# Reordering the first loads and conversions of a Fourier-mixing and hardswish kernel on one core

## Chip, cores and metric

The kernel runs on one core of a Trainium2 chip. The metric is the device time of one execution in microseconds (us); lower is better. The core has five engines with a queue of instructions each: TensorE (PE; PEld is its weight load), VectorE (DVE), ScalarE (ACT), GpSimd (POOL) and SyncE (SP). SP, ACT and POOL also issue DMA transfers, which run on 16 shared DMA engines.

## The reference

```python
def _attn_ref(x) -> np.ndarray:               # x: (8, 3008, 256) float32
    X = np.fft.fft(x, axis=1)
    X = np.fft.fft(X, axis=2)
    return X.real.astype(np.float32)

def _moe_ref(x, w_in, w_out) -> np.ndarray:   # x: (24064, 256), w_in: (256, 2048), w_out: (2048, 256)
    h = x @ w_in
    relu6 = np.clip(h + 3.0, 0.0, 6.0)
    g = h * relu6 / 6.0
    return (g @ w_out).astype(np.float32)
```

The second function takes the first one's result, reshaped to (24064, 256). x is float32; both weight matrices arrive as float64.

## The kernel before

**Stages.** The sequence of 3008 is split as 47 x 64 (`N1`, `N2`). Stage 1 is the transform over the 47, as products with the table `F`; x is first folded, that is, added to its mirrored partner (`fold_half`, `fold_columns`), so that half the products are left. Its results `z` go out to DRAM (`zd`) and come back in another layout as groups `g`. Stage 2 is the transform over the 64, with the table `T`, and gives `q`. The transform over the 256 features is not run on the data: `fold_w_in` multiplies it (table `C`) into `w_in`, which gives `W1`; the last row of the result is kept as a column per feature block, `WN`. From `q`, `W1` and `WN` come the hidden values: `mlp1_products` makes two products `u` and `v` on TensorE, and `activate` adds them, the row `qn` times `WN` (L544) among them, and applies the hardswish on VectorE and ScalarE. The second product uses seven products in place of eight per 2 x 2 block (`G`, `combine`, `mlp2`, `finish`). The batch is worked in four pairs (`pairs`), each in chunks, each chunk in eight steps (`NF`).

**Float64 weights.** No engine multiplies float64 here, so each weight piece (512 KB, 16 in all: `PIECES`) is taken apart by hand. `load_w(j)` loads it on POOL's queue. `exponent_a(j)` writes the exponent's bytes into `PM[j % 3]` (two ScalarE instructions, L745), `exponent_b(j)` adds them up by two products on TensorE (L757), `exponent_c(j)` scales them on ScalarE (L760). `mantissa(j)` builds the fraction on VectorE (L768, L769), `join(j)` multiplies both there (L777 for pieces of `w_in`, L783 for `w_out`). Pieces 0 and 1 are the first two of `w_in`, 2 and 3 of `w_out`, 4 and 5 of `w_in` again, and so on. `fold_w_in(j)` then makes eight products, copies the result to `W1` (L811) and issues the `WN` transfers on SP (L815): 128 numbers of one partition to one number in each of 128 partitions.

**Order.** The order on each engine is the order in which the program's text issues things (`manual_schedule`). The start reads, from L828: TensorE runs `keep_awake` fillers (products of ones with zeros, L826); SP loads `FI`, `first_slot`, `C`, `F` (L833 to L837); POOL loads weight pieces 0 and 1 (L881), then issues eight gathers of x for the first half batch (`load_half`, L174, indices `IX` from `FI`), then pieces 2 and 3. ScalarE and VectorE convert pieces 0 and 1 as far as they can, ScalarE copies `first_slot` into the last x tile (L893) and clears a part of `T`, and SP loads the first part of `T` (`load_t(0)`, L895). Four rounds follow (`ORDER`), each with a fold on VectorE and its products in `stage1_early`; the last round is the one in `SPLIT`. `load_g_half` brings back the first group. `see` is a tiny POOL copy of a number of that group: POOL waits there, so the loads of pieces 4 to 9 behind it start when the group has landed. Then come the rest of the first conversions, `fold_w_in(0)` and `(1)`, stage 2 of the first group (`stage2_half`, its copy at L448, and `spread_by_pe` for `qn`), and the first products. `starting[0]` is true up to there.

**First steps.** For the first eight steps, `first_steps` and `second_steps` alternate and weave in the conversion of the pieces left. `head_b(j)` is `mantissa(j)` followed by the load of a later piece (`NEXT`: 6 loads 12, 7 loads 13, 8 loads 14, 9 loads 15). Behind these steps the loop runs `mlp1`, `combine` and `mlp2` evenly.

Of the kernel before, what the change touches and what calls it, by code (L numbers as in the profile page):

```python
# [58 lines left out]
def kernel(  # L59
# [140 lines left out]
    def fold_columns(hb, m, j, eng):  # L200
        a, r = hb.x[m][0:PX - 1, j::2, :], hb.xr[m][0:PX - 1, XC - 1 - j::-2, :]
        for p, q in ((slice(0, P + 1, P), slice(0, P + 1, P)), (slice(1, P), slice(D - 1, P, -1)),
                     (slice(D - 1, P, -1), slice(1, P))):
            eng.tensor_tensor(a[:, :, p], a[:, :, p], r[:, :, q], op=AL.add)
# [512 lines left out]
    def load_w(j):  # L717
        kind, n, i = PIECES[j]

        pool, tag, bufs = (wpool, "st", 2) if j in STRAIGHT else (spool, "t", None) if j in (2, 3) else (xpool, "x", None)  # L720
        st = pool.tile([P, 2 * WB], I32, tag=tag, bufs=bufs, name="st")
        o = st[:].bitcast(moe_w_in.dtype)
        if kind == "in":
            cs = slice(in_column(n, i), in_column(n, i) + WB // 2)
            nc.gpsimd.dma_start(out=o.rearrange("p (c j) -> p c j", c=2),
                                in_=moe_w_in[:, cs].rearrange("(c p) f -> p c f", p=P))
        else:
            r = (2 * n + i * NF) * P
            nc.gpsimd.dma_start(out=o.rearrange("p (c j) -> p c j", c=2),
                                in_=moe_w_out[r:r + 2 * P, :].rearrange("(c p) d -> p c d", p=P))  # L730
        raw[j] = st
# [9 lines left out]
    def exponent_a(j):  # L741
        top = raw[j][:].bitcast(I16).rearrange("p (n four) -> p n four", four=4)[:, :, 3]
        for i in range(2):
            low = PM[j % len(PM)][:, i].bitcast(U8).rearrange("p (n two) -> p n two", two=2)[:, :, 0]
            nc.scalar.activation(low, top, AF.Identity, bias=bias[:, i:i + 1], scale=(1 - 2 * i) / 16.0)  # L745

    def exponent_b(j):
        pm = [PM[j % len(PM)][:, i].bitcast(F16) for i in range(2)]
        if starting[0]:
            exs[j] = ps_h.tile([P, WB], F32, tag="uv", name="ex")[:]  # L750
        elif j % 2 == 0:
            exs[j] = bank([P, WB], "ex")[:]
        else:

            exs[j] = spare[1 if j % 4 == 1 else 0][:].rearrange("p i n -> p (i n)")
        for i in range(2):
            nc.tensor.matmul(exs[j], E[:, i], pm[i], start=(i == 0), stop=(i == 1))  # L757

    def exponent_c(j):
        nc.scalar.activation(exs[j].bitcast(I32), exs[j], AF.Identity, scale=2.0 ** 23)  # L760

    def mantissa(j):
        st = raw[j]
        hi = st[:].rearrange("p (n two) -> p n two", two=2)[:, :, 1]
        lo = st[:].bitcast(U32).rearrange("p (n two) -> p n two", two=2)[:, :, 0]
        top = wpool.tile([P, WB], I32, tag="top", bufs=3, name="top")
        frac = top[:].bitcast(F32)
        nc.vector.tensor_scalar(top[:], hi, 0xFFFFF, 0x100000, op0=AL.bitwise_and, op1=AL.bitwise_or)  # L768
        nc.vector.scalar_tensor_tensor(frac, lo, 2.0 ** -32, top[:], op0=AL.mult, op1=AL.add)  # L769
        fracs[j] = frac  # L770

    def join(j):
        kind, n, i = PIECES[j]
        frac, ex = fracs.pop(j), exs.pop(j)
        if kind == "in":
            o = wpool.tile([P, WB], F32, tag="wi", bufs=4, name="wi")
            nc.vector.tensor_tensor(o[:], frac, ex, op=AL.mult)  # L777
            w[PIECES[j]] = o[:]
            return

        for h, g in enumerate((B21, B22) if i else (B11, B12)):
            f, e = (t.rearrange("p (c q h e) -> h p c q e", c=2, h=2, e=DH)[h] for t in (frac, ex))
            nc.vector.tensor_tensor(block(n, g).rearrange("p c (q e) -> p c q e", e=DH), f, e, op=AL.mult)  # L783
# [15 lines left out]
    def fold_w_in(j):  # L799

        _, n, k = PIECES[j]
        nb = WB // 2
        cs = slice(in_column(n, k), in_column(n, k) + nb)
        wi = w.pop(PIECES[j]).rearrange("p (i f) -> p i f", i=2)

        ps = bank([P, 2, nb], "wps") if starting[0] else spare[k]
        for blk in range(2):
            for i in range(2):
                nc.tensor.matmul(ps[:, blk], C[:, i, blk * P:(blk + 1) * P], wi[:, i], start=(i == 0), stop=(i == 1))
        fs = range(cs.start // P, cs.stop // P)  # L810
        nc.scalar.copy(W1[:, :, cs], ps[:])  # L811

        wait = [] if k else fs[1:]
        for f in [fs[0], *rest, *(() if wait else fs[1:])]:
            nc.sync.dma_start(out=WN[:, f:f + 1], in_=W1[P - 1:P, 1, f * P:(f + 1) * P])  # L815
        rest[:] = wait

    def load_t(gr, ks=slice(0, 2 * KK)):
        for b in range(2):
            nc.sync.dma_start(out=T[b * N2:(b + 1) * N2, b, gr, :, ks], in_=c_stage2[:, gr, :, ks])  # L820


    def keep_awake(n, by=None):
        ps = ps_d.tile([P, 2 * TB], F32, tag="d", name="awake")
        for i in range(n):
            nc.tensor.matmul(ps[:], ones[:], Z[:] if by is None else by, start=True, stop=True)  # L826
# [1 line left out]
    Z = spool.tile([P, 2 * TB], F32, tag="s", name="Z")  # L828
    nc.vector.memset(Z[:], 0.0)
    nc.vector.memset(ones[:], 1.0)  # L830
    keep_awake(11)
    hb = halves[0]
    nc.sync.dma_start(out=FI[:], in_=c_stage1[:, 7 * PB:])  # L833
    first_slot = qpool.tile([P, 2 * TB], F32, tag="qn", name="first_slot")
    load_zero(first_slot[PB:PB + N1, 0:D], hb, nc.sync)
    nc.sync.dma_start(out=C[:], in_=c_dim.rearrange("(h p) d -> p h d", p=P))
    nc.sync.dma_start(out=F[:], in_=c_stage1[:, 0:7 * PB])  # L837
    bias = wpool.tile([P, 2], F32, tag="bias", name="bias")
    for i in range(2):
        nc.vector.memset(bias[:, i:i + 1], (2 * i - 1) * 7.5 / 16.0 - 896.0)  # L840
# [25 lines left out]
    def head_b(j):  # L866
        mantissa(j)
        if j in NEXT:
            load_w(NEXT[j])

    def tail(j):
        exponent_c(j)
        join(j)


    def see(x):
        nc.gpsimd.tensor_copy(seen[:], x)

    for j in range(2):  # L881
        load_w(j)
    nc.gpsimd.affine_select(E[:, 0], ones[:], pattern=[[-1, P]], compare_op=AL.is_equal, fill=0.0, base=0,
                            channel_multiplier=1)
    nc.scalar.mul(E[:, 1], E[:, 0], -1.0)
    for k, m in enumerate(ORDER):
        load_half(hb, m)
    for j in range(2, 4):
        load_w(j)
    for j in range(2):  # L890
        exponent_a(j)
        mantissa(j)
    nc.scalar.copy(zero_slot(hb), first_slot[PB:PB + N1, 0:D])  # L893
    clear_table(1)
    load_t(0)  # L895
    for k, m in enumerate(ORDER):
        if m in SPLIT:
            for j in range(2):
                fold_columns(hb, m, j, nc.vector)
        for part in range(2) if m not in SPLIT else ():  # L900
            fold_half(hb, m, part, nc.vector)
        stage1_early(hb, m)
    later[:] = later[4:6] + later[0:4] + later[6:8]
    load_g_half(hb, 0)

# [4 lines left out]
    take_half(halves[1], ORDER[0], cpool, "c")  # L910
    load_half(halves[1], ORDER[0])

    mantissa(2)
    for j in range(2):
        exponent_b(j)
        exponent_c(j)
        join(j)
    keep_awake(2)
    exponent_a(2)
    fold_w_in(0)  # L920
    exponent_a(3)
    fold_w_in(1)
    mantissa(3)
    exponent_b(2)
    keep_awake(1)
    exponent_b(3)
    tail(2)

    stage2_half(hb, 0)
    spread_by_pe(hb, bank([P, TB], "ps3")[:])  # L930
    tail(3)
    starting[0] = False
    spare = [ps_a.tile([P, 2, WB // 2], F32, tag="acc", name="spare") for h in range(2)]
# [114 lines left out]
    def second_steps(s):  # L1048
        j = 2 * s + 4
        if j - 2 < len(PIECES):  # L1050
            head_b(j)
            join(j)
            head_b(j + 1)
            if s == 1:
                mlp2_first(*chunk(s), halves=(0,))
                exponent_b(j + 1)
            exponent_c(j + 1)
            if j + 2 < len(PIECES):
                head(j + 2)
            join(j + 1)  # L1060
            if j + 3 < len(PIECES):
                exponent_a(j + 3)
                if s > 1:
                    head_b(j + 3)
            if s > 1:
                mlp2_first(*chunk(s), halves=(0,))
            if s == 3:
                stage2_half(halves[0], 1)
            mlp1(*chunk(s + 1))
            if s == 1:  # L1070
                head_b(j + 3)
            return
        mlp1(*chunk(s + 1))
        combine(*chunk(s + 1))
        mlp2_first(*chunk(s), halves=(0,))
        mlp1(*chunk(s + 2))
        mlp2_first(*chunk(s), halves=(1,))
# [117 lines left out]
```

## Time and profile before

| What | us |
|---|---|
| median of three runs (1944.76 to 1946.93) | 1946.17 |
| the profiled execution | 1950.4 |
| its span, from first to last instruction | 1948.7 |
| TensorE busy in it | 1928.2 |
| VectorE busy | 1425.6 |
| GpSimd busy | 1440.8 |
| ScalarE busy | 680.8 |
| first fold starts (VectorE) | 14.16 |
| stage 1's last product ends (TensorE) | 30.45 |
| first group back (POOL's `see`) | 36.81 |
| first product of `mlp1` (TensorE) | 41.56 |
| first product of the second step's `v` (TensorE) | 49.75 |

Times inside an execution count from the start of the span. The profile's groups and waits are read thus: a line of the kernel, the engine and its operation, what it wrote and read, how many there were, their busy time, and the idle time of the engine ahead of them with what ended it. The granted clock is the share of full speed that TensorE was given.

### The profile page before, as it was taken

To read this page: it belongs to the slowest core of one execution; us is meant where nothing else is said; L and a number is where in the kernel's file an instruction comes from. 1 tells how busy PE (TensorE), PEld (TensorE's weight loads), DVE (VectorE), ACT (ScalarE), POOL (GpSimd) and SP (SyncE) were. 2 spreads that over 40 slices of the span, in tenths; PEclk is the share of its full clock that TensorE was granted. 3 is DMA by queue.
4 is the path that set the end of the run, shared out by engine and by line. 5 is a ranking of instruction groups with operands and counts; after the bars stand their busy time and mean duration, and the time that the engine had idled before them with its cause. 6 is when DMAs were issued, how large, how long until landed. Compare 5 with 4: busy or idle time off the path is not lost.

```text
span 1948.7 us, 28199 instructions
## 1 busy us (share of the span) xinstructions
PE 1928.2 (99%) x9362; PEld 1660.2 (85%) x9362; DVE 1425.6 (73%) x2759; ACT 680.8 (35%) x1166; POOL 1440.8 (74%) x1646
## 2 busy tenths in 40 slices
PE   8999999999999999999999999999999999999998
PEld 5578888888998888888898888888899888888887
DVE  4877776767777777777787777777778777777777
ACT  4633333333333333333333333333333333333332
POOL 3487888886688887787678887878667667666765
PEclk8999999999999999999999999999999999999999
DMA  6431223311112122121111221212110101101000
GB/s 231 149 98 36 66 60 82 76 47 35 36 31 55 45 73 68 39 55 29 40 36 43 57 57 43 50 50 54 35 28 20 28 17 26 33 14 28 20 20 20
DMA packets 154600, 98.77 MB, mean 51 GB/s; under 512 B 121877, under 2 KB 136062, under 8 KB 154454
## 3 DMA queue, kind: packets, MB, share of 16 engines
q1 hardware_dynamic: 142562, 57.97, 12.3%
q0 software_dynamic: 11184, 38.77, 6.8%
q8 instruction: 73, 1.20, 0.3%
q14 instruction: 73, 0.60, 0.1%
q10 hardware_dynamic: 708, 0.23, 0.1%
HBM read 59.61 MB, written 37.32 MB: 50 GB/s over the span
## 4 chain that ended last, share of the span: by engine, by line
PE 94%; DVE 3%; DMA 1%; ACT 1%; issue 0%; POOL 0%; DVEq 0%; SPq 0%; ACTq 0%; POOLq 0%
PE acc L628 56%; PE v L535 16%; PE u L535 16%; PE ps L484 2%; PE ps L279 1%; PE acc L608 1%; DVE a L584 1%; DMA WN<-W 1%; DVE s L544 1%; ACT t L581 1%; DMA xt<-in_x_dram,IX 0%; PE ps L342 0%; DVE o L689 0%; DVE u L565 0%; PE ps L445 0%
## 5 line engine op out<-in xcount | busy, mean ns | idle before, releaser
L598 POOL TENSOR_TENSOR c<-a 128x512 f32<-128x512 f32 (+1 forms) x375 | 469.1, 1251 | 359.7 <-PE acc L628 304.2
L628 PE MATMUL acc<-c,G 128*128 128x256 f32 (+1 forms) x3008 | 697.2, 375 | 0.0
L581 ACT ACTIVATE t<-u,half 128x512 f32<-128x512 f32 (+1 forms) x384 | 260.6, 679 | 1148.4 <-DVE u L554 1069.1
L628 PEld LDWEIGHTS acc<-c,G 128*128 128x128 f32 x3008 | 565.2, 190 | 71.6 <-POOL c L598 0.4
L544 DVE SCALAR_TENSOR_TENSOR s<-qn,WN,u 128x256 f32<-128x256 f32 (+1 forms) x768 | 330.7, 472 | 344.0 <-PE u L535 337.1
L628 PE MATMUL acc<-a,G 128*128 128x256 f32 (+1 forms) x2256 | 541.6, 375 | 0.0
L628 PEld LDWEIGHTS acc<-a,G 128*128 128x128 f32 x2256 | 421.0, 189 | 73.6 <-issue 20.2
L535 PE MATMUL v<-q,W 127*128 127x256 f32 (+1 forms) x1536 | 389.4, 375 | 4.9 <-DVE a L584 4.9
L535 PE MATMUL u<-q,W 128*128 128x256 f32 (+1 forms) x1536 | 388.0, 375 | 0.2 <-ACT q L448 0.2
L584 DVE SCALAR_TENSOR_TENSOR a<-t,u 128x512 f32<-128x512 f32 (+2 forms) x448 | 264.1, 601 | 101.0 <-ACT t L581 96.1
L535 PEld LDWEIGHTS v<-q,W 127*128 127x128 f32 x1536 | 287.9, 190 | 46.3 <-DVE a L584 6.4
L535 PEld LDWEIGHTS u<-q,W 128*128 128x128 f32 x1536 | 285.8, 190 | 36.9 <-issue 1.9
L598 POOL TENSOR_TENSOR c<-a,c 128x256 f32<-128x256 f32 (+1 forms) x375 | 268.5, 716 | 29.4
L598 POOL TENSOR_TENSOR c<-c,a 128x256 f32<-128x256 f32 (+1 forms) x375 | 268.4, 716 | 29.4
L554 DVE TENSOR_TENSOR u<-s,v 128x512 f32<-128x512 f32 x352 | 245.0, 696 | 37.8 <-DVE s L544 0.9
L584 DVE SCALAR_TENSOR_TENSOR a<-t,v 128x512 f32<-128x512 f32 (+1 forms) x480 | 263.7, 566 | 0.1
L581 ACT ACTIVATE t<-v,half 128x512 f32<-128x512 f32 (+1 forms) x384 | 260.6, 679 | 0.2 <-PE acc L628 0.2
L556 DVE TENSOR_TENSOR v<-v,s 128x512 f32<-128x512 f32 x352 | 243.9, 693 | 0.0
L598 POOL TENSOR_TENSOR r<-w,e 128x256 f32<-128x256 f32 (+1 forms) x92 | 88.7, 985 | 3.6
L638 ACT ACTIVATE e<-acc 128x512 f32<-128x512 f32 (+2 forms) x184 | 83.4, 544 | 0.0
L689 DVE STREAM_TRANSPOSE o<-r 128x256 f32<-128x256 f32 (+1 forms) x192 | 72.6, 416 | 0.2
L598 POOL TENSOR_TENSOR w<-w,e 128x512 f32<-128x512 f32 (+1 forms) x46 | 57.5, 1250 | 3.6
(130 smaller groups left out, 797.7 us busy)
## 6 DMA issues: line engine op xcount, KB each, us to landing
out_dram<-o SPq DMA_DIRECT2D x747, 32.0 KB
g<-zd SPq DMA_DIRECT2D x42, 256.0 KB
zd<-z SPq DMA_DIRECT2D x48, 192.0 KB
xt<-in_x_dram POOLq DMA_DIRECT2D x21, 256.0 KB
st<-in_moe_w_in_dram POOLq DMA_DIRECT2D x8, 512.0 KB
st<-in_moe_w_out_dram POOLq DMA_DIRECT2D x8, 512.0 KB
qn<-qd SPq DMA_DIRECT2D x16, 256.0 KB
xt<-in_x_dram POOLq DMA_DIRECT2D x17, 192.0 KB
```

Of the source, the lines that this page charges most:

```text
L279: nc.tensor.matmul(ps[b][h * PB:(h + 1) * PB, 0:n], F[rows(b), 0:PB], y[rows(b), 2 * h:2 * h + n], start=True, stop=not last, skip_group_c ...
L484: nc.tensor.matmul(ps[:, blk, u * P:n].rearrange("p (b k) -> p b k", b=2), g[:, kk, blk * (P + 1):blk * (P + 1) + P], T[:, :, gr, blk, kk, ...
L535: nc.tensor.matmul(ps[:, i, 0:nq], W1[r, blk, f * P:(f + 1) * P], q[r, blk, of:of + nq], start=True, stop=True)
L544: nc.vector.scalar_tensor_tensor(s[:, i, 0:nq], qn[:, of:of + nq], WN[:, f:f + 1], u[:, i, 0:nq], op0=AL.mult, op1=AL.add)
L554: nc.vector.tensor_tensor(u[:], s[:], v[:], op=AL.add)
L556: nc.vector.tensor_tensor(v[:], v[:], s[:], op=AL.subtract)
L581: nc.scalar.activation(t, h, AF.Relu, bias=half[:], scale=scale)
L584: nc.vector.scalar_tensor_tensor(dst, t, 1.0, h, op0=AL.min, op1=AL.mult)
L598: (eng or nc.gpsimd).tensor_tensor(out, in0, in1, op=AL.add)
L628: nc.tensor.matmul(ch.acc[i // 2][:, i % 2, 0:ch.n], G[:, i, fc, :], mv, start=(fc == 0 and i % 2 == 0), stop=(fc == NF - 1), skip_group_c ...
L638: nc.scalar.mul(ch.e[:, k:i + 1, 0:ch.n], ch.acc[i // 2][:, 0:i + 1 - k, 0:ch.n], 1.0 / WS)
L689: nc.vector.transpose(o[:, 0:n // DH, h], ch.r[:, m, h, 0:n].rearrange("p (j i) -> p j i", i=DH))
```

## The change

Nothing of the computation differs; instructions are issued in another order, on another engine, or left out (fillers).

- SP loads `F` and `C` ahead of `first_slot`, and `load_t(0)` is issued behind the second round of stage 1.
- POOL loads only weight piece 0 ahead of the gathers of x; pieces 1, 2 and 3 come behind them.
- Two filler products fewer at the start (`keep_awake(9)` in place of 11).
- `exponent_a(1)` and `mantissa(1)` move back: the mantissa into the last round, behind its `fold_columns`, the exponent behind stage 1.
- Behind stage 1 the conversions of pieces 0 to 3 are interleaved in another order, and the first two copies to `W1` are made by VectorE.
- In the second step (`s == 1` in `second_steps`), POOL first makes a `see` of one of the new `WN` columns, and only then loads pieces 12 and up.

```diff
-        nc.scalar.copy(W1[:, :, cs], ps[:])
+        (nc.vector.tensor_copy if starting[0] else nc.scalar.copy)(W1[:, :, cs], ps[:])
...
-    keep_awake(11)
+    keep_awake(9)
     hb = halves[0]
     nc.sync.dma_start(out=FI[:], in_=c_stage1[:, 7 * PB:])
+    nc.sync.dma_start(out=F[:], in_=c_stage1[:, 0:7 * PB])
+    nc.sync.dma_start(out=C[:], in_=c_dim.rearrange("(h p) d -> p h d", p=P))
     first_slot = qpool.tile([P, 2 * TB], F32, tag="qn", name="first_slot")
     load_zero(first_slot[PB:PB + N1, 0:D], hb, nc.sync)
-    nc.sync.dma_start(out=C[:], in_=c_dim.rearrange("(h p) d -> p h d", p=P))
-    nc.sync.dma_start(out=F[:], in_=c_stage1[:, 0:7 * PB])
...
-    for j in range(2):
-        load_w(j)
+    load_w(0)
...
     for k, m in enumerate(ORDER):
         load_half(hb, m)
-    for j in range(2, 4):
+    for j in range(1, 4):
         load_w(j)
-    for j in range(2):
-        exponent_a(j)
-        mantissa(j)
+    exponent_a(0)
+    mantissa(0)
     nc.scalar.copy(zero_slot(hb), first_slot[PB:PB + N1, 0:D])
     clear_table(1)
-    load_t(0)
     for k, m in enumerate(ORDER):
         if m in SPLIT:
             for j in range(2):
                 fold_columns(hb, m, j, nc.vector)
+            mantissa(1)
         for part in range(2) if m not in SPLIT else ():
             fold_half(hb, m, part, nc.vector)
         stage1_early(hb, m)
+        if k == 1:
+            load_t(0)
...
+    exponent_b(0)
+    exponent_c(0)
     mantissa(2)
-    for j in range(2):
-        exponent_b(j)
-        exponent_c(j)
-        join(j)
+    join(0)
+    exponent_a(1)
     keep_awake(2)
+    mantissa(3)
+    exponent_b(1)
+    exponent_c(1)
+    join(1)
     exponent_a(2)
     fold_w_in(0)
+    fold_w_in(1)
+    exponent_b(2)
+    exponent_c(2)
     exponent_a(3)
-    fold_w_in(1)
-    mantissa(3)
-    exponent_b(2)
     keep_awake(1)
-    exponent_b(3)
-    tail(2)
+    join(2)
 
     stage2_half(hb, 0)
     spread_by_pe(hb, bank([P, TB], "ps3")[:])
+    exponent_b(3)
     tail(3)
...
         if j - 2 < len(PIECES):
+            if s == 1:
+                see(WN[:, NF + 2:NF + 3])
             head_b(j)
```

## The prediction

> **What bounds the kernel now.** I read the page first. TensorE is busy 99% of the span, and the chain that ended last is almost all TensorE. Only the first of the forty slices (each 48.7 us) has gaps, and the change touches only code that runs in the first 85 us. The products behind it are not altered, so the question is how much earlier TensorE reaches its gapless stretch.
>
> ```profile
> span 1948.7 us, 28199 instructions
> PE   8999999999999999999999999999999999999998
> PE 94%; DVE 3%; DMA 1%; ACT 1%; issue 0%; POOL 0%; DVEq 0%; SPq 0%; ACTq 0%; POOLq 0%
> ```
>
> Next I read the chain of waits over the first 200 us, in order of time (start, us, what).
>
> ```profile
> 5.02 9.04 DMA xt<-in_x_dram,IX
> 14.06 0.03 issue
> 14.11 0.05 issue
> 14.16 0.56 DVE xt L215
> ...
> 17.84 0.26 PE pt L321
> ...
> 38.96 7.51 DMA WN<-W
> 46.50 0.49 DVE s L544
> ...
> 62.37 4.01 DMA WN<-W
> 66.40 0.49 DVE s L544
> ```
>
> The chain has three DMA waits: the first pair of x gathers (landed at 14.06), the weight column `WN` for the first products (46.50), and the next such column (66.40). Between 17.84 and 30.45 it is TensorE without a gap, so stage 1, once fed, sets its own length.
>
> Then the table by stretches (us, busy time of PE, PEld, DVE, ACT, POOL, then TensorE's granted clock, DMA share, GB/s) for what the transfers do ahead of x, and TensorE's own table by half microseconds for the clock.
>
> ```profile
> 6.00:10.00 4.00, 4.00 (x10) 1.86 (x9) 0.83 (x2) 0.80 (x2) 2.82 (x3) 1.00 1.02 291
> 10.00:14.00 4.00, 3.77 (x9) 1.33 (x7) 1.41 (x3) 3.17 (x5) 3.35 (x4) 1.00 1.03 408
> ```
>
> ```profile
> 16.50:17.00 0.50, 0.00 (x0) 0.74 1.06 418
> 17.00:17.50 0.50, 0.40 (x8) 0.50 1.02 410
> ```
>
> The DMA engines are full ahead of x, so x comes when the bytes in front of it are through. TensorE's clock falls to half at about 16.7, before stage 1 starts, and stays there until 33.8. Last, the timeline, for who waits.
>
> ```profile
> 1.37 1.68 POOL L725 DMA_DIRECT2D st<-in_moe_w_in_dram  x2 [0.84 <-POOLq L1179]
> 30.49 0.69 DVE L350 COPY z<-ps 112x512 f32<-112x512 f32 x1 [7.04 <-PE ps L342]
> 36.81 0.18 POOL L877 COPY seen<-g 128x1 f32<-128x1 f32 x1 [21.44 <-DMA g<-zd]
> 40.92 0.58 ACT L448 COPY q<-ps 128x512 f32<-128x512 f32 x1 [1.50 <-PE ps L445]
> 49.75 1.13 PE L535 MATMUL v<-q,W 127*128 127x256 f32 x4 [2.76 <-DVE a L584]
> ```
>
> **Part 1: less ahead of x.** `load_w(1)` (512 KB) moves behind the eight gathers and `load_t(0)` (two transfers of 128 KB) behind the second stage-1 group: 786,432 bytes less ahead of the first pair. At 408 GB/s that is 1.93 us, at 291 GB/s 2.70 us. The two weight pieces were taken up by VectorE at 9.13 and 11.35, so they landed 2.2 us apart: the second one crossed mostly in the slow stretch. I take 2.4 us. [...] POOL's issue allows it: one issue of 0.84 us falls away ahead of the gathers, but they also need `IX`, ready at 3.06, so the first goes out about 0.5 us earlier (3.65 before). If issue and not bytes set the landing, the gain would be 0.5 us: the low end. Before, 8.1 us lay between the second gather's last issue (5.99) and the landing, while the pair gathered at 90 us landed 4.5 us after its last issue (92.3 to 96.8), so bytes set it.
>
> VectorE's folds (14.16 to 23.45 without a gap) then start near 11.75, and stage 1 near 15.4. The later pairs follow at 1.05 MB/408 GB/s = 2.57 us each, near 14.2, 16.8 and 19.4; VectorE asks for them 2.4 us ahead of 17.82, 19.27 and 21.88, thus at 15.4, 16.9 and 19.5: just in time. Stage 1 ends 2.4 us earlier.
>
> The other moved steps on SP: F and C go ahead of `first_slot`, whose issue moves back 0.9 us. Its copy (L893, 0.40 us) is first read by the fold at 15.68, 1.5 us behind the start of folding; this is its cover, and without it each microsecond of lateness costs one. `load_t(0)` issues 2 x 0.61 us on SP behind the stores that ran from 25.35 to 26.6; the next stores came at 27.86, so they wait at most a few tenths, and the last one, which matters, not at all. The table is first read at 39.6, some 10 us later.
>
> **Part 2: fillers.** `keep_awake(9)` for 11 takes four passes of 0.43 us away: TensorE goes idle at 12.06, not 13.77, and stage 1 asks at 14.7 instead of 17.10. The idle gap is about 2.6 us for 3.3. Cost nothing, as the clock is at half in stage 1 already.
>
> **Part 3: the conversions behind stage 1.** `mantissa(1)` (0.43 + 0.69 us) goes into VectorE's 7.04 us of waiting ahead of L350. `exponent_a(1)` (2 x 0.71 us) now stands on ScalarE behind stage 1. Counting from stage 1's end (30.45 before): ScalarE's store issue to +1.5, `exponent_c(0)` to +2.1, `exponent_a(1)` to +3.55; TensorE fills that time with `exponent_b(0)` (0.85 at half clock) and `keep_awake(2)` (2.75), so `exponent_b(1)` goes at about +3.6 to +4.2, where the fillers ended +4.35 before. Then ScalarE +4.85, `join(1)` (0.68) +5.6, the two folds (8 products each, 1.74 and 1.75) to +7.7, VectorE's copy (0.69 instead of ScalarE's 0.58) +8.4, and the second `WN` transfer goes out at +8.5; before, 38.96 is +8.5. Without the fillers' cover it would be up to 1.4 us later. The copy of q follows `exponent_b(2)` +8.2, `exponent_c(2)` +8.85, `exponent_a(3)` +10.3: before, 40.92 is +10.5. So it is zero by rows; I let it vary by 1 us either way with the clock. The group lands at +6.4 as before and sends off six weight pieces, so `WN`'s 7.5 us, spent beside them, stay. Everything to 62 us moves by 2.4.
>
> **Part 4: `see` at step 1.** POOL now waits for WN[:, NF+2] before it loads piece 12. That transfer went out at 62.37 and took 4.01 us; the table shows no traffic from 58 to 63, and piece 12, issued at 61.91, after. The nearest row for a small transfer alone is FI: 1.82 us from issue (0.82) to the end of `IX`'s wait (2.64). Landed at 64.2 to 64.9, it is in time for VectorE, which stood still 0.99 us ahead of 66.40 and has no gap of that size from there to 87. Bounds: 0 (the 4 us are not piece 12's doing) and 0.99; I take 1.0, since TensorE too waits 1.10 for VectorE there and runs full behind it. Behind the wait on POOL are the loads of 12 to 14, up to 2.7 us later; the first is read at 78.7, ten microseconds after it lands. If that cover were gone, the wait would cost what it gives.
>
> **Sum.** 2.4 + 1.0 = 3.4 us. The profiled execution took 1950.4 (span 1948.7, 1.7 around it), so 1947.0; the median of the runs, 1946.17, lies 4.2 below it, which gives **1942.8**. With 1.93 to 2.7 for x, 0 to 1 for `see` and 0.7 either way for the clock: 1941.3 to 1944.9.
>
> **Rivals.**
> *Stage 1 runs warm.* The gap shrinks to 2.6 us. TensorE then would not be the bound of stage 1: VectorE's folds end at 21.05, and half of the last group's 5.45 us (25.0 to 30.45) at full clock, 1.4 to 2.7 us, follows; stage 1 ends at 22.5 to 23.8 instead of 28.05, some 4.5 us more: 1938.3. Against it: the gap of 2.76 us at 47.0 also dropped the clock (0.50 from 51.0), and stage 1's small products (47 rows, 64 columns) didn't raise it in ten gapless microseconds. [...] Chance 0.1.
>
> *The shift is mostly swallowed.* Issue on POOL sets the landing, 0.5 us, and `see` gives 1.0: 1944.7. For it: the gathers' issue period, 1.25 to 1.3 us, is as long as their transfer; against it the 8.1 us above. Or `see` gives nothing: 1943.8. Chance 0.22.
>
> *Slower: the clock is down through both folds.* Its place is TensorE between stage 1 and the `WN` transfer. Stage 1 ends 2.4 us earlier, but the clock rose at 33.8 after 3.4 gapless microseconds from 30.4, and such a rise may come later if the dense stretch begins in the midst of whatever the clock counts by. At half clock all through: 28.05 + 0.85 + 3.42 (filler) + 0.85 + 6.84 (16 products of 0.43) = 40.0, copy 0.7, `WN` out at 40.75, 1.8 us later than before, while the weight pieces go out 2.4 us earlier and are ahead of it. It decides when it eats more than 2.4 + 1.0; landing 1.8 late and with `see` no help, +1.8: 1948.0. Against it: a dense stretch raised the clock in 3.4 us there and from 50.9 to 54.2. Chance 0.1.
>
> *It doesn't do what it says:* W1's later arrival could stop VectorE at `mantissa(1)`; it lands 1.3 us (512 KB at 408 GB/s) behind the last pair, near 20.7, and is asked for at 21.05, with 7 us of cover, so it's part of the swallowed case.
>
> **How the numbers follow.** Forecast 0.56, warm 0.1, swallowed 0.22, slower 0.1, others 0.02. 0.2% is 3.9 us, about what a measurement of this kernel can tell: faster means under 1942.3, slower over 1950.1. A good third of the forecast's own range, all of the warm case: 0.3 faster. Most of the rest is within: 0.63; slower 0.07, as the slow case must come worse than worked out. The range runs from 1939.6 (part of the warm case left out) to 1946.8 (part of the slow one).
>
> **What would show it.** The first fold near 11.7 (x), TensorE's last stage-1 product near 28.0, the first activation's wait for `WN` over near 44.1, no VectorE wait for `WN` near 63, the gapless stretch of TensorE from about 82.6 instead of 86. I am wrong if folding starts after 13, if the clock is at 1.0 within stage 1, or if `WN` goes out more than 9 us behind stage 1.

## The result, and the profile after

| What | before, us | after, us |
|---|---|---|
| median of the runs (7 each, run together) | 1946.93 (1944.74 to 1947.74) | 1940.45 (1936.18 to 1942.23) |
| the profiled execution | 1950.4 | 1940.88 |
| its span | 1948.7 | 1939.2 |
| first fold starts (VectorE) | 14.16 | 11.08 |
| stage 1 starts / ends (TensorE) | 17.84 / 30.45 | 14.77 / 26.57 |
| first group back (POOL's `see`) | 36.81 | 32.95 |
| first product of the second step's `v` (TensorE) | 49.75 | 42.65 |

The time after is 0.9966 of the time before (95%: 0.9954 to 0.9977), that is 6.5 us less; 3.4 us were forecast. The profiled pair lies further apart, 9.5 us, because the execution of before that was profiled is 3.5 us over its median and that of after 0.4 us over.

The page of the changed kernel: the span, TensorE's busy tenths in the forty slices, and the engines' shares of the chain that ended last.

```profile
span 1939.2 us, 28196 instructions
PE   9999999999999999999999999999999999999998
PE 94%; DVE 3%; POOL 1%; ACT 1%; DMA 1%; issue 0%; DVEq 0%; ACTq 0%; POOLq 0%
```

Only the first slice differs: it now reaches 9. Everything gained is in the first 85 us. The chain of waits of the changed kernel there (start, us, what):

```profile
4.45 6.53 DMA xt<-in_x_dram,IX
...
11.08 0.56 DVE xt L215
...
14.77 0.21 PE pt L321
...
24.21 2.36 PE ps L342 x32
26.57 0.97 PE ex L757 x2
...
34.84 4.95 DMA WN<-W
...
42.65 1.13 PE v L535 x4
```

The gathers are awaited 6.53 us instead of 9.04, stage 1 follows 3.1 us earlier, the `WN` wait behind `fold_w_in` is 4.95 us instead of 7.51, and the third DMA wait of before (62.37) is gone. The timeline of the changed kernel shows the waits from the waiting engine's side (start, us, engine and operation, and in brackets the idle time ahead with what ended it):

```profile
39.81 0.48 DVE L544 SCALAR_TENSOR_TENSOR s<-qn,WN,u 128x256 f32<-128x256 f32 x1 [0.88 <-DMA WN<-W]
...
42.65 1.13 PE L535 MATMUL v<-q,W 127*128 127x256 f32 x4 [0.23 <-DVE a L584]
...
55.61 0.18 POOL L877 COPY seen<-WN 128x1 f32<-128x1 f32 x1 [8.99 <-DVE top L769]
56.13 0.87 DVE L544 SCALAR_TENSOR_TENSOR s<-qn,WN,u 128x256 f32<-128x256 f32 x2
```

The first of these lines in the kernel before:

```profile
46.50 0.48 DVE L544 SCALAR_TENSOR_TENSOR s<-qn,WN,u 128x256 f32<-128x256 f32 x1 [3.05 <-DMA WN<-W]
```

VectorE waits 0.88 us for the first `WN`, 3.05 before, and TensorE's idle time at the second step's `v`, 2.76 us before, is down to 0.23. The new `see` stands at 55.61, and the two multiplications by `WN` behind it run as one pair with no wait between them. Last, TensorE's table by half microseconds (us, PE busy (instructions), granted clock, DMA share, GB/s):

```profile
15.50:16.00 0.50, 0.50 (x8) 0.66 1.04 426
16.00:16.50 0.50, 0.50 (x10) 0.50 1.09 410
...
29.00:29.50 0.50, 0.50 (x2) 0.69 0.63 148
29.50:30.00 0.50, 0.50 (x2) 1.00 0.00 0
```

The clock still falls, but at 15.7, when stage 1 has run for 0.9 us, and not ahead of it; it rises at 29.3. There is no second fall here; before, the clock was also down from 50.9 to 54.3.

Step by step, the profiled pair draws apart as follows: 3.1 us at the first fold; 0.8 more by the end of stage 1; 0.2 more when `WN` goes out (34.84 against 38.96); 2.6 in the `WN` wait; 0.4 to the second step's `v`; 1.7 by the next pair of multiplications by `WN` (47.79 against 56.59), which is the missing second fall of the clock; 1.1 at the `WN` wait that fell away. That makes 9.9 us at the step that began at 86.04 and begins at 76.15 now, of which 9.5 reach the end.

### The profile page after: what moved, and what is told of

Its sections match the earlier page's. It is cut to its first block, busy times and chain, and to the rows that moved or that the text cites. A ratio compares the mean times of both kernels' runs of the same rounds, so it can differ in the third digit from the quotient of the medians.

```text
span 1939.2 us, 28196 instructions
## 1 busy us (share of the span) xinstructions
PE 1923.2 (99%) x9358; PEld 1657.9 (85%) x9358; DVE 1427.0 (74%) x2761; ACT 679.8 (35%) x1164; POOL 1440.6 (74%) x1647
## 4 chain that ended last, share of the span: by engine, by line
PE 94%; DVE 3%; POOL 1%; ACT 1%; DMA 1%; issue 0%; DVEq 0%; ACTq 0%; POOLq 0%
PE acc L628 56%; PE v L535 16%; PE u L535 16%; PE ps L484 2%; PE ps L279 1%; PE acc L608 1%; DVE a L584 1%; ACT t L581 1%; DVE s L544 1%; POOL c L598 0%; PE ps L342 0%; PE spare L809 0%; DMA xt<-in_x_dram,IX 0%; DVE o L689 0%; PE ps L445 0%
```

## Experiments

**Theories.** *A (the terms of the sum):* the transfers ahead of x and the `see` give what was worked out, and the rest is scatter between executions. *B (the clock):* the surplus comes from TensorE's clock, which depends on where TensorE is idle. *C (a shorter `WN` wait):* the new order behind stage 1, costed at zero, is worth something by itself. The first four ran on one chip beside 29 runs of the kernel before (median 1945.9, 1943.91 to 1948.86), the next four on another beside 9 (1947.26), the last three on a third beside 17 (1947.72). In all these 55 runs of the kernel before, the clock's mean was 0.993 to 0.995.

### The kernel before, once more

No edit. 

> The kernel before, unchanged, to see how single runs and their granted clocks differ. Its profiled execution took 1950.4 us, 3.5 over the median of seven runs (1946.93). Theory A (the first start of TensorE's gapless stretch is set by x, by the WN column and by the wait in the second step): runs stay within 1944 to 1948, mean clock near 0.993 in all. [...]

1946.27 us (11 runs, 1944.70 to 1949.59), ratio 1.0002 (0.9993 to 1.0011). In its profile the first fold starts at 13.75, the clock is down from 16.4 to 33.4 and from 50.5 to 53.9, and the timeline has the same idle time of TensorE as before:

```profile
49.13 1.13 PE L535 MATMUL v<-q,W 127*128 127x256 f32 x4 [2.53 <-DVE a L584]
```

So both falls of the clock and this gap came in both profiled executions. These two lie 3.5 and 3.3 us over their medians, though, with a clock's mean of 0.993; 62 of the 66 runs of this kernel on the three chips (these 11 and the 55) have 0.994 or 0.995, that is less time at half clock. How many of them have the second fall is not shown. The times pass A's bound of 1948 and the clock's mean differs by 0.002 between runs, which speaks for B, but time and clock go together only loosely here (1944.70 and 1947.89 both at 0.995).

### The changed kernel, once more

No edit. 

> The changed kernel, unchanged. Its seven runs fall into two groups: 1936.2 and 1936.7 us with a mean clock of 0.998 to 0.999, and 1939.9 to 1942.2 with 0.995 to 0.996. Theory B: runs of both groups again, none in between, and where the profile falls in the fast group stage 1 shows a granted clock of 1.0 throughout. Theory A alone: one group near 1940, the same clock.

1942.10 us (12 runs, 1936.17 to 1946.21), ratio 0.9982 (0.9973 to 0.9990): 3.8 us less here. The runs fall into two groups by the clock's mean: 1936.17 and 1937.81 at 0.999 and 0.998, and ten at 0.994 to 0.996, from 1940.24 to 1946.21 (their median 1942.46). In the first series it was the same: 1936.18 and 1936.73 at 0.999 and 0.998, five from 1939.93 to 1942.23 (median 1940.88). The run that was profiled is the one of 1936.17; TensorE's table by half microseconds:

```profile
12.50:13.00 0.50, 0.06 (x1) 1.00 0.92 352
13.00:13.50 0.50, 0.00 (x0) 1.00 1.00 410
...
16.50:17.00 0.50, 0.50 (x19) 1.00 1.02 418
...
21.00:21.50 0.50, 0.50 (x35) 1.00 0.98 349
```

The fillers end at 12.6, TensorE is idle for 1.79 us, the clock never falls, and stage 1 makes up to 35 products in half a microsecond where at half clock it made 7 to 20. Its last product ends at 22.6 instead of 26.6. This is the rival "stage 1 runs warm", in 4 of 19 executions. A alone can't explain two groups.

### Without the `see` at step 1

```diff
-            if s == 1:
-                see(WN[:, NF + 2:NF + 3])
```

> The changed kernel without the tiny POOL copy that waits for WN in the second step. My theory: VectorE again waits about 1.0 us for WN ahead of the third step, and the time is 1.0 us above the changed kernel's. Rival: the WN transfer is early enough anyway, then nothing changes (within 0.3 us).

1943.74 us (11 runs, 1941.33 to 1945.81), all at 0.994 to 0.996, against 1942.46 for the changed kernel's runs at that clock: 1.3 us, a rough figure, as single runs lie 4.5 us apart. In the timeline the wait for `WN` is back:

```profile
58.86 0.48 DVE L544 SCALAR_TENSOR_TENSOR s<-qn,WN,u 128x256 f32<-128x256 f32 x1 [0.88 <-DMA WN<-W]
```

The `WN` transfer took 3.88 us on the chain (4.01 before). So the `see` does what it was said to do, at about the price given for it (1.0).

### Three fillers more in the changed kernel

```diff
-    keep_awake(9)
+    keep_awake(12)
```

> The changed kernel with 12 filler products at the start instead of 9; TensorE then works until 14.1 us, where the first product of stage 1 comes (14.03), so the 2.5 us gap is gone. Theory B with stage 1's small products holding a clock that is up: clock 1.0 through stage 1 in every run, 1936 us in all, mean clock 0.998 or more. [...] Third: nothing changes, as VectorE's folds feed stage 1 anyway.

1936.28 us (5 runs, 1936.07 to 1936.70), ratio 0.9952 (0.9940 to 0.9965), the clock's mean 0.998 to 0.999 in every run. The only edit is work for TensorE ahead of stage 1, which fills the gap there; the time is that of the changed kernel's warm executions, now each time. B holds, and this version beats both kernels. Its chain behind stage 1:

```profile
22.03 0.99 PE ps L342 x32
...
25.14 1.33 ACT PM L745 x2
...
26.50 0.38 PE ex L757
26.88 3.45 PE wps L809 x16
```

Stage 1 ends at 23.0, and the folds of the weights now wait for `exponent_a(1)` on ScalarE (L745).

### The kernel before with four fillers more

```diff
-    keep_awake(11)
+    keep_awake(15)
```

> The kernel before with 15 filler products at its start instead of 11: TensorE works to about 17.2 us, where its first stage-1 product comes (17.10), so the 3.3 us gap is gone, and nothing else differs. Theory (the gap alone drops the clock, and stage 1's small products hold it once it is up): clock 1.0 through stage 1, stage 1 ends about 11.2 us behind the first fold (as in the warm execution of the changed kernel: 11.41 to 22.63) instead of 16.3, so near 25.4, and the time is about 5 us less: 1941, with a spread under 2 us if the later wait for WN drops no clock. Rival (the filler only pays together with the earlier x): within 1 us of the kernel before.

1939.07 us (5 runs, 1938.48 to 1939.38), ratio 0.9959 (0.9945 to 0.9972), clock 0.998 to 0.999. Four fillers alone take 8.2 us off the kernel before, more than the whole change does. Stage 1 ends at 25.1 (25.4 expected); the time was expected near 1941 and came 2 us lower. The second fall of the clock went too, which the expectation had left open, and so did VectorE's wait for the first `WN`.

### The same with the `see` alone

```diff
-    keep_awake(11)
+    keep_awake(15)
...
+            if s == 1:
+                see(WN[:, NF + 2:NF + 3])
```

> The kernel before with 15 fillers and the POOL wait alone. If the wait is worth 1.0 us here too: 1.0 below the kernel before with 15 fillers. What then is left between this one and the kernel with the old loads and the new conversions is the price of the new order of conversions: zero by my count of instructions, rival 1 us either way.

1938.02 us (5 runs, 1937.25 to 1938.20): the `see` is worth 1.05 us by itself, with everything else as before. Its chain behind stage 1, the old order of conversions at full clock:

```profile
26.16 0.59 ACT ex L760
26.77 0.70 DVE wi L777
27.52 3.72 PE wps L809 x16
```

### The changed kernel with the old loads, warm

The order of the loads and tables as before, all else as changed, and fillers up to stage 1.

```diff
-    keep_awake(9)
+    keep_awake(15)
...
-    load_w(0)
+    for j in range(2):
+        load_w(j)
...
-    for j in range(1, 4):
+    for j in range(2, 4):
         load_w(j)
...
+    load_t(0)
...
-        if k == 1:
-            load_t(0)
```

(`C` and `F` stand behind `first_slot` again, too.) 

> The changed kernel with the old order of the loads (both weight pieces, the tables and T ahead of x) and 15 fillers; the new order of the conversions and the POOL wait stay. If the earlier x is worth the 3.1 us by which folding started earlier: 1936.3 + 3.1 = 1939.4. Rival: with stage 1 no longer TensorE's, part of the 3.1 us is lost to the later pairs of x, and it is 1938 or less.

1939.13 us (5 runs, 1938.81 to 1939.47). Against the kernel before with `see` and fillers it differs only in the order of the conversions (with VectorE making the first two copies to `W1`), and is 1.1 us slower. Its chain shows why:

```profile
26.66 0.58 ACT ex L760
27.24 1.32 ACT PM L745 x2
28.60 0.38 PE ex L757
28.98 3.45 PE wps L809 x16
```

The folds begin 3.8 us behind VectorE's copy of stage 1 (25.15); in the old order 2.9 us (24.65 to 27.52). The 1.32 us of `exponent_a(1)` stand on the chain: at full clock the four fillers take 1.88 us, not 2.7, and no longer hide it.

### Warm, with the new loads, without the `see`

```diff
-    keep_awake(9)
+    keep_awake(12)
...
-            if s == 1:
-                see(WN[:, NF + 2:NF + 3])
```

> The changed kernel with 12 fillers and without the small POOL copy that waits for WN. With the clock up from run to run the same, the price of this part alone shows: 1.0 us over the 1936.3 with the copy, from VectorE's wait ahead of the third step. Rival: no difference, and the 1.6 us between the medians without it and with it (1943.74 and 1942.10) were the clock's scatter.

1937.23 us (5 runs, 1936.80 to 1939.08), where 1937.3 was expected. With the 1.05 us for the `see`, the new loads are worth 1939.13 - 1937.23 + 1.05 = 2.95 us on this chip, all at the same clock (2.85 against the version with 12 fillers on the first chip). The profiled run is its slowest; its first fold starts at 12.66, the latest of all seven profiles with the new loads, which shows how far x alone varies.

### `exponent_a(1)` ahead of the end of stage 1

The version with 12 fillers, with `exponent_a(1)` issued in the last round. Behind stage 1 the conversions of pieces 0 to 3 stand as in the kernel before again (but for an earlier `mantissa(3)`), so two things change at once.

```diff
-    keep_awake(9)
+    keep_awake(12)
...
             mantissa(1)
+            exponent_a(1)
...
-    exponent_b(0)
-    exponent_c(0)
...
-    join(0)
-    exponent_a(1)
+    for j in range(2):
+        exponent_b(j)
+        exponent_c(j)
+        join(j)
     keep_awake(2)
+    exponent_a(2)
     mantissa(3)
-    exponent_b(1)
-    exponent_c(1)
-    join(1)
-    exponent_a(2)
     fold_w_in(0)
+    exponent_a(3)
     fold_w_in(1)
     exponent_b(2)
-    exponent_c(2)
-    exponent_a(3)
     keep_awake(1)
-    join(2)
+    exponent_b(3)
+    tail(2)
...
-    exponent_b(3)
     tail(3)
```

> The changed kernel with 12 fillers, and the exponent of piece 1 made in the last round of stage 1 (beside its mantissa) instead of behind it; both exponents' products follow stage 1 at once. With the old loads the new order of conversions cost 1.1 us (1939.13 against 1938.02), and the chain of waits there runs through exponent_a(1), 1.32 us. Theory: that is its whole price, and this kernel is about 1.0 us faster than the 1936.28: 1935.3. Rival: ScalarE now works 1.4 us ahead of the last round's copies, the group comes back that much later, and nothing is gained.

1936.15 us (5 runs, 1935.86 to 1936.67), where 1935.3 was expected: 0.1 us better than with 12 fillers alone, within the scatter (and that version ran on another chip). From its chain:

```profile
20.95 0.59 ACT z L350
21.54 1.32 ACT PM L745 x2
...
25.57 3.72 PE wps L809 x16
...
31.94 0.59 ACT q L448
32.58 1.13 PE u L535 x4
...
38.01 0.86 PE v L535 x4
```

The folds start 14.3 us behind the first fold of x (11.30), against 15.1 with 12 fillers alone (11.82 to 26.88). So 0.8 us is gained there. By the second step's `v` only 0.15 us of it is left (26.71 us behind the first fold, against 26.86): the folds take 3.72 us instead of 3.45, and the first `u` waits for ScalarE's copy of q (L448), in whose time TensorE had products of `exponent_b(3)` in the other version. So the expectation fell, and not by its rival: the group comes back no later (18.35 us behind the first fold, 18.50 with 12 fillers alone). The early exponent alone, with the new order, was not tried.

### The changed kernel with the old loads and the old number of fillers

The loads as in the warm version above, with `keep_awake(11)`. 

> The changed kernel with the old order of the loads and the old 11 fillers, so with the clock left to itself. The order of conversions costs nothing here if the fillers behind stage 1 run at half clock and hide exponent_a(1) (2.75 us then, 1.88 us at full clock); left is the POOL wait: 1.0 us under the kernel before. Rival: 1.1 us lost and 1.0 gained, no change.

1944.68 us (11 runs, 1943.79 to 1947.28), clock 0.994 to 0.995, against 1947.72: 3.0 us less by the medians without any of the new loads, where 1.0 was expected; the ratio, 0.9990 (0.9982 to 0.9999), says 2 us (0.2 to 3.5). The `see` accounts for 1.05, which leaves some 1 to 2 us, and nothing at the low end of the interval. The timeline shows where they can come from:

```profile
42.99 0.48 DVE L544 SCALAR_TENSOR_TENSOR s<-qn,WN,u 128x256 f32<-128x256 f32 x1 [0.51 <-DMA WN<-W]
```

VectorE's wait for the first `WN` is 0.51 us instead of 2.8 to 3.05, TensorE is not idle at the second step, and the clock does not fall a second time (it is down once, 18.0 to 31.6). So C holds for the waits in the profiles. In the time the new order of conversions is worth 1 to 2 us at half clock, as far as these runs can tell, and at full clock it costs 1.1.

### One filler more in the changed kernel

```diff
-    keep_awake(9)
+    keep_awake(10)
```

> The changed kernel with 10 fillers instead of 9: the gap ahead of stage 1 is about 1.7 us instead of 2.5. The profiled executions of the changed kernel: clock down with a gap of 2.5 us, up with one of 1.5 us. [...]

1942.28 us (6 runs): one at 1936.91 (0.998), five from 1941.34 to 1944.47 (0.994 to 0.995). So the shorter gap did not bring all runs near 1936: one of 6 came there, and 4 of 19 with 9 fillers. The profile is of one of the five (1942.72):

```profile
12.50:13.00 0.50, 0.34 (x1) 1.00 1.01 344
...
14.00:14.50 0.50, 0.34 (x8) 1.00 1.05 410
...
16.50:17.00 0.50, 0.50 (x17) 0.61 1.03 418
```

The gap ahead of the first small products (1.32 us) is shorter than the 1.79 us of the warm execution above, and yet the clock fell at 16.6. So shortening the gap from 2.51 us to 1.32 did not keep the clock up here, and the gap's length alone doesn't tell these two executions apart.

### The terms together

| Term | forecast | measured |
|---|---|---|
| new loads (x earlier) | 2.4 (1.93 to 2.7) | 2.3 at the first fold (mean of 7 profiles 11.56, of 6 with the old loads 13.88); 2.85 to 2.95 in the time |
| `see` at step 1 | 1.0 (0 to 0.99) | 1.05 warm, 1.1 in the profiled pair, 1.3 at half clock |
| order of the conversions | 0, up to 1.4 lost without the fillers' cover | 1 to 2 gained at half clock, 1.1 lost at full clock |
| clock | 0.7 either way | 4 of 19 runs without the fall (by the clock's mean): 4.4 to 5.5 us less than the others |

The first three rows add up to 5 to 6 us for an execution at half clock. The changed kernel's runs at that clock lay 6.1 us under the kernel before in the first series and 3.4 in the second, so the sum fits the one and not the other; why is open.

## Why the prediction was right, and where it was mis-sized

**Direction, range, x and `see`: right.** The median of the first series, 1940.45, lies within 1939.6 to 1946.8, and that of the second, 1942.10, is 0.7 from the forecast. That it comes so near is luck in part: the sum lacks the terms below. Of the signs that the prediction named, the first fold came at 11.08 (11.7 forecast) and the wait near 63 went; stage 1 ended at 26.57 (28.0), and the first wait for `WN` at 39.81 (44.1), earlier than the sum had it. One of its signs of being wrong came as well: the clock at 1.0 within stage 1, for 0.9 us in the profiled execution, throughout in the warm one. The bytes ahead of x set its landing, as argued from the 8.1 us behind the last issue: had POOL's issue set it, the first fold would have come 0.5 us earlier and not 2.3. The 2.4 us that I took mostly from the row of the slow stretch (291 GB/s) were near it. The whole effect in the time is some 0.5 us over the term; I can't say from these runs where that half microsecond comes from.

**"`WN`'s 7.5 us, spent beside them, stay": wrong, and the largest missing term.** With the new order this wait was 4.95 us in the profiled pair, 5.97 without the `see`, 6.64 with one filler more, and with the old loads too VectorE stood still only 0.51 us. I had argued that six weight pieces go out at the same place relative to it, and so they nearly do (the `WN` transfer leaves 1.39 us behind the first piece's issue, 1.65 before). But a few tenths seem to count. Over the 13 profiles the transfer took at most 5.0 us wherever it left up to 1.40 us behind the first piece, and 6.0 to 7.5 us, up to the end of VectorE's wait, in the four where it left 1.50 to 2.44 us behind. Old and new order stand on both sides: with the old order and the clock up (the two kernels before with 15 fillers, 0.3 us behind) VectorE did not wait at all. So the new order by itself does not make the transfer shorter; its place next to the pieces goes with it. Why remains open; no run altered the pieces and the `WN` transfer separately.

**What hung on it was not in the sum at all.** I used the 2.76 us of idle TensorE at 47.0 as evidence on the clock, but did not ask what becomes of that gap itself. It shrank to 0.23 (1.27 and 1.93 in two other profiles of the new order), and in none of them did the clock fall behind it; in both profiles of the kernel before it did, after 2.76 and 2.53. At half clock L608's four products there took 3.46 us instead of 1.88. Where gap and second fall both went, with the old loads, that is 2.6 and 1.6 us by the profiles; 1 to 2 of it reached the time, and the chain there also runs through `exponent_a(1)` (1.33 us), which the clock, up again at 31.6, uncovers.

**"Cost nothing, as the clock is at half in stage 1 already": wrong in its reason.** Part 2 took the clock before as given. Stage 1 came forward by 3.1 us, but the fall of the clock only from 16.7 to 15.7, so its first 0.9 us ran at full speed (0.8 us in the profiled pair), and in 4 of 19 executions the fall did not come. Against the warm rival I held that stage 1's small products had not raised the clock in ten gapless microseconds. That is true and doesn't bear on it: with 12 and 15 fillers the same products ran at a clock of 1.00 throughout. The rival's 1938.3 was also too high (1936.2 to 1937.8), as it was built on a sum without the two terms above.

**The conversions "zero by rows": right up to the issue of `WN`, and at half clock only.** It went out 8.3 us behind the end of stage 1, where +8.5 was worked out; what was wrong is what followed. The cover that I named, the fillers at half clock, is what decides: warm, the order costs 1.1 us of the 1.4 that I gave for that case.

**The profiled execution.** The sum was made against an execution 3.5 us over the later median; taking it off as a whole was right for the median, but it means that the profiled pair overstates the change (9.5 against 6.5, and 3.8 in the second series).

**The slower rival** (clock down through both folds) did not happen: the clock rose at 29.3, before the 16 products of the folds began at 30.6.

## What to carry to other kernels

Ask of every gap on TensorE not only what it costs but whether the clock falls behind it, and close it with filler products up to the first real one: here three or four fillers were worth more than the whole reordering, and made the time steady (0.9 and 0.6 us between runs, where the same kernels without them had 5.1 and 10.0). Where a moved step has its cost hidden by work whose length goes with the clock, cost it at both clocks. And let bulk loads wait for the tiny transfers that somebody else waits for: one copy of one column as a gate gave 1 us here.

## What the runs showed of the hardware

**When the clock changed.** Read off the half-microsecond tables (a slice's mean clock gives the moment within it), the clock of the kernel before fell at 16.74, rose at 33.81, fell at 50.88 and rose at 54.29: 17.07, 17.07 and 3.41 apart. Its second profile gives 17.07, 17.06 and 3.41. The changed kernel's clock was down for 13.65 (15.66 to 29.31), as was that of three of its variants (13.65 or 13.66). What sets these times is not shown by the runs. The rows of the kernel before behind the fall at 16.74:

```profile
33.50:34.00 0.50, 0.50 (x2) 0.69 0.00 0
50.50:51.00 0.50, 0.50 (x3) 0.88 0.57 229
54.00:54.50 0.50, 0.50 (x3) 0.71 0.71 213
```

**The fillers change their pace, and not at the same time in each execution.** In the kernel before one pass starts every 0.85 us up to 6.11 and every 0.43 us from 6.74 on, in the changed kernel every 0.85 us up to 5.25 and every 0.43 us from 5.77 on (the tables show a clock of 1.00 from the start of the span). The traces' records of the clock begin there, at 6.50 and 5.42, and in both profiles the clock fell 10.24 us later, at 16.74 and 15.66. The same 18 passes take 9.84 us in the profiled execution of the changed kernel and end at 11.52, and take 10.89 us in the warm one and end at 12.57:

```profile
1.68 9.84 PE L826 MATMUL awake<-Z,ones 128*128 128x512 f32 x18 [1.68 <-DVE ones L830]
1.68 10.89 PE L826 MATMUL awake<-Z,ones 128*128 128x512 f32 x18 [1.68 <-DVE ones L830]
```

The gap ahead of the first product of stage 1 was 2.51 us in the one, with the clock's fall at 15.66, and 1.79 us in the other, without one. Whether the time of the change of pace goes with the two groups of times is not shown: one execution of the warm group was profiled.

**Gaps of 1.3 to 2.8 us, with and without a fall.** After a gap of 1.32 us ahead of sparse products the clock fell in one profile (10 fillers, at 16.61), after one of 1.79 us it didn't in another (the warm one), and after gaps of 2.53 and 2.76 us ahead of dense ones it fell both times (at 50.49 and 50.88, in the two profiles of the kernel before). How much work keeps the clock up is not settled by these runs.

**Stage 1's products at both clocks.** Its products of 47 rows and 64 columns stood at 0.50 from 17.8 to 30.4 without a gap in the kernel before, and the clock did not rise there; they ran at 1.00 throughout in the warm execution and in four profiles with 12 or 15 fillers (1.00 from 12 to 60 us); in the profiled execution of the changed kernel the clock fell from 1.00 to 0.50 at 15.66, 0.9 us behind their start.
